# A list scheduler that takes Pool and VectorE's SBUF-only work as one resource, a second engine for the ELU's middle step, and one batch more with its first queries in front

## The chip, the cores and the metric

One core of a Trainium2 chip runs the kernel. The metric is the device time of one execution in microseconds; the kernel before takes 1211.21 us (median of three runs, 1208.86 to 1212.19). The engines are named as in the profile: PE is TensorE's matmuls and PEld its weight loads, DVE is VectorE, ACT is ScalarE, POOL is GpSimd, SP is SyncE, whose queue issues all the DMAs here.

## The reference

Attention with a decay bias over 8 batches, 8 heads, 576 positions of 64 values, and then a feed-forward layer with an ELU over the 4608 resulting rows of 512 values:

```
scores = q @ k.T / sqrt(64)                       # per batch and head, causal
bias   = -(cum[query] - cum[key]),  cum = cumsum(max(s, 0))
attn   = softmax(where(causal, -1e9, scores + min(bias, 0)))
x      = (attn @ v), heads side by side           # 4608 x 512
h      = x @ w_in                                 # 512 -> 2048
g      = where(h > 0, h, exp(min(h, 0)) - 1)
out    = g @ w_out                                # 2048 -> 512
```

The weights arrive as 64-bit floats and are rebuilt on the chip as 32-bit ones. All products keep nearly full float32 accuracy: an operand is split into a rounded high part and a rest (names ending in h and l), and three products of parts replace one.

## The kernel before

**The attention.** The 576 queries of a batch are one half block of 64 and four blocks of 128 (`NQ` = 4). There are two ways to do them. For the first `N_CUT` = 3 batches the first 320 queries (the half block and two blocks, `CUT` = 2) of each pair of heads are one `Low` unit: it works in plain float32, four passes per matmul, and needs few vector steps (`prepare_low`, `scoring_low`, `weighing_low`; on PE the tiles `sc<-kl,ql`, `trl` for transposes, `avl`). These 12 units, three batches of four pairs of heads, come first. I call them the front. All other queries are done in `Unit`s with split operands: for a batch that was cut, blocks 2 and 3 of each head (late units); for an uncut batch, per pair of heads, one unit for the two half blocks (its tiles have `None` in the name) and one per head for all four blocks. A `Unit` needs more vector work: L353 and L351 round q and k, L363 and L362 take the rests, L841 reduces the scores from PSUM, L846 is the exponential, and then each block of probabilities is scaled and split into two 16-bit parts (`halved`). The high part is written by POOL (L891), DVE (L893) or ACT (L895); the low part by DVE in one instruction (L899) or by POOL in two (L885, then L886). SP then loads the parts back transposed (`T<-p`, L344), and PE multiplies them with v (L969).

**The feed-forward part.** The rows, in the order in which they are finished, make 12 chunks of 384 (`moe_chunk`). For each chunk, 16 slices f of 128 hidden values follow each other. `hidden(f)` is 12 matmuls of 384 columns (L1131) into one of two PSUM banks `h`. Then comes the ELU: ACT writes exp(h) to the single buffer `g` (L1139), DVE takes min(g, 1) - 1 in place (L1140), DVE adds max(h, 0) from PSUM (L1142), and this frees the bank; one of POOL, ACT and DVE rounds `g` to `gh` (L351, L353, L355), and POOL or DVE takes the rest `gl` (L363, L362), which frees `g`. `project(f)` is 9 matmuls of 512 columns (L1155).

**The order.** None of this is written in the order in which it runs. Each step is an `op` with a priority, its reads and writes, and one or more ways: an engine, an estimated cost in ns, and the code. `Plan.issue` is a list scheduler: again and again it takes the step that can start first by its own estimates, ties by priority, and puts it on the way that ends first. A way's cost counts times `BIAS` when ways are compared, 2 for DVE. What it fixes is the order on each engine; on the chip every engine runs its list in order and waits for semaphores. Attention units have priorities from 0 on (10 more for each `Low` unit, 5 more for each other), weights `W0 + WD * f` = 60 + 5 f, the vector steps of the feed-forward part -1000 and its matmuls 10000, so that they fill what PE has left. The planner counts POOL and DVE as independent of each other.

Of the kernel before, what the change touches and what calls it, by code (L numbers as in the profile page):

```python
# [31 lines left out]
W0, WD = 60, 5  # L32
# [9 lines left out]
N_CUT, CUT = 3, 2  # L42
# [29 lines left out]
class Plan:  # L72
# [18 lines left out]
    BIAS = {"DVE": 2.0}  # L91
# [59 lines left out]
    def issue(self):  # L151
        engines = sorted({w[0] for o in self.ops for w in o.ways})
# [17 lines left out]
        while pending:  # L170
# [3 lines left out]
            for o in pending:  # L174
# [97 lines left out]
def dve_1(n):  # L272

    return 165 + 0.7 * n


def dve_2(n):

    return 150 + 1.5 * n
# [11 lines left out]
def kernel(  # L291
# [55 lines left out]
    def rounded(prio, n, dst, src, reads, writes, sign=1.0, only=None):  # L347

        ways = [
            ("Pool", pool_1(n),  # L350
             lambda: pool.tensor_scalar(dst(), src(), sign, 1.0, ALU.mult, ALU.mult)),  # L351
            ("ACT", act_s(n),
             lambda: act.activation(dst(), src(), AF.Copy, scale=sign)),  # L353
            ("DVE", dve_1(n),
             lambda: dve.tensor_scalar(dst(), src(), sign, None, ALU.mult)),  # L355
        ]
        op(prio, [w for w in ways if only is None or w[0] in only], reads, writes)

    def rest(prio, n, dst, src, hi, reads, writes, only=None):

        ways = [
            ("DVE", dve_2(n), lambda: dve.tensor_tensor(dst(), src(), hi(), ALU.subtract)),  # L362
            ("Pool", pool_2(n), lambda: pool.tensor_tensor(dst(), src(), hi(), ALU.subtract)),  # L363
        ]
        op(prio, [w for w in ways if only is None or w[0] in only], reads, writes)
# [31 lines left out]
    def decay_sums():  # L397
# [14 lines left out]
        op(-9, [("DVE", 1900.0, sums)], [], [(aux, 0), (aux, 1)])  # L412
        op(-5, [("DVE", 1300.0, parts)], [(aux, 0)], [(aux, 1), (aux, 2)])
# [57 lines left out]
    def load_unit(f, kind, src, parts):  # L471
# [7 lines left out]
        if wide:  # L479
# [11 lines left out]
                ("DVE", 500.0, lambda: dve.tensor_scalar(  # L491
# [3 lines left out]
            op(prio, [("DVE", 500.0, lambda: dve.tensor_scalar(  # L495
# [3 lines left out]
            def gather():  # L499
                dve.scalar_tensor_tensor(  # L500
                    raw.v[:, :, 0], raw.v[:, :, 1], 0x80000000, raw.v[:, :, 0],
                    ALU.bitwise_and, ALU.bitwise_or,
                )
                dve.scalar_tensor_tensor(
                    raw.v[:, :, 0], raw.v[:, :, 1], 3, raw.v[:, :, 0],
                    ALU.logical_shift_left, ALU.bitwise_or,
                )

            op(prio, [("DVE", 1450.0, gather)], [(raw, 1)], [(raw, 0)])
# [317 lines left out]
    def softmax_block(prio, tag, native, pt, w, mask, mv, reads, operands, inv, view=lambda v: v):  # L827
# [21 lines left out]
        if last:  # L849
            def inverse():  # L850
                dve.tensor_scalar(sm.v[:, :ns], sm.v[:, :ns], EPS, 1.0 / up, ALU.add, ALU.mult)  # L851
                dve.reciprocal(sm.v[:, :ns], sm.v[:, :ns])  # L852

            op(prio, [("DVE", 350.0, inverse)], [], [sm])

    def normalize(prio, pt, w, sm, col):
# [4 lines left out]
            ("DVE", 220 + 0.7 * w, lambda: dve.tensor_scalar(  # L861
# [5 lines left out]
    def halved(u, i, pt, sm, col):  # L867
# [20 lines left out]
        for part, n in ((whole, k * P), (rest, HB))[: 1 + (i == u.last)]:  # L888
# [4 lines left out]
                ("DVE", 220 + 0.7 * n, lambda part=part: dve.tensor_scalar(  # L893
# [5 lines left out]
                ("DVE", dve_2(n), lambda part=part: dve.scalar_tensor_tensor(  # L899
# [211 lines left out]
    def moe_chunk(ch, rows, xc, after):  # L1111
# [13 lines left out]
        def hidden(f):  # L1125
            hp = plan.buf(ps, [P, TMAX], F32, f"h_{ch}_{f}", tag="h", bufs=N_H)
            for c in range(NCB):
# [12 lines left out]
            op(side, [("DVE", dve_1(TC), lambda: dve.tensor_scalar(  # L1140
                g.v[:, :TC], g.v[:, :TC], 1.0, -1.0, ALU.min, ALU.add))], [], [g])
            op(side, [("DVE", dve_p(TC), lambda: dve.scalar_tensor_tensor(  # L1142
                g.v[:, :TC], hp.v[:, :TC], 0.0, g.v[:, :TC], ALU.max, ALU.add))], [hp], [g])
# [134 lines left out]
```

## Time and profile before

| | before |
|---|---|
| median of 3 runs | 1211.21 us |
| the profiled execution, device time | 1205.16 us |
| its span in the trace | 1203.4 us |
| DMA, mean rate | 130 GB/s |

The profiled execution is 6.05 us (0.5%) under the median, and 1.8 us of its device time lie outside the span. Rows of the trace give start, duration, engine, line and the tiles written and read. A group's row gives a count, its busy time, the mean of one in ns, and the idle time of its engine just before it with what ended it. In float32 each matmul of a `Low` unit stands as two records. A wait of one engine for a port of another is not a wait in these views: it lengthens the instruction that waits.

### The profile page before, as it was taken

How to read it: one execution, taken by the hardware profiler on the slowest of the kernel's cores; microseconds unless marked ns; L12 is line 12 of the kernel's file. 1: busy time of each engine (PE TensorE's matmuls, PEld its weight loads, DVE VectorE, ACT ScalarE, POOL GpSimd, SP SyncE). 2: the span in 40 equal slices, each digit the busy share in tenths (PEclk: the TensorE clock that was granted, in tenths of full speed). 3: DMA queues.
4: the chain of work that ended last, by engine and by line, in shares of the span. 5: the costliest groups of instructions: out<-in, count | busy, mean ns of one | idle time of the engine just before them, and what ended most of it. 6: DMA issues, size and time to landing. Idle time of an engine off the chain costs nothing. (4 is left out here: it accounts for less than half of the span.)

```text
span 1203.4 us, 19946 instructions
## 1 busy us (share of the span) xinstructions
PE 1117.1 (93%) x5992; PEld 950.5 (79%) x5992; DVE 859.7 (71%) x1903; ACT 608.9 (51%) x1500; POOL 819.5 (68%) x996
## 2 busy tenths in 40 slices
PE   5788887999999999999999999999999999999998
PEld 4577766778787778878878888878877887899996
DVE  6879999899877778768787777777787777422221
ACT  4676445554555554655555555445554554332322
POOL 6787888787877656867787777777776776332322
PEclk9899899999999999999999999999999999999999
DMA  7766566867676476566576565575665565210000
GB/s 197 205 160 201 156 153 150 194 146 150 162 155 129 103 167 125 123 157 128 127 170 139 122 165 128 130 172 122 128 149 129 123 140 128 60 53 1 27 1 27
DMA packets 342316, 156.55 MB, mean 130 GB/s; under 512 B 267560, under 2 KB 321088, under 8 KB 342208
## 3 DMA queue, kind: packets, MB, share of 16 engines
q1 hardware_dynamic: 342208, 155.27, 55.6%
q8 instruction: 48, 0.79, 0.3%
q14 instruction: 60, 0.49, 0.1%
HBM read 79.66 MB, written 19.32 MB: 82 GB/s over the span
## 5 line engine op out<-in xcount | busy, mean ns | idle before, releaser
L1131 PE MATMUL h<-xh,wi 128*128 128x384 f32 x1536 | 446.6, 341 | 9.7 <-DVE g L1142 9.6
L1155 PE MATMUL o<-wo,gh 128*128 128x512 f32 x1152 | 363.8, 397 | 2.2 <-DVE mn L841 1.5
L1131 PEld LDWEIGHTS h<-xh,wi 128*128 128x128 f32 x1536 | 284.4, 189 | 20.4 <-DVE g L1142 11.7
L363 POOL TENSOR_TENSOR gl<-g,gh 128x384 fp32r<-128x384 f32 x157 | 169.7, 1081 | 158.2 <-ACT gh L353 134.5
L1131 PE MATMUL h<-xl,wi 128*128 128x384 f32 x768 | 260.2, 339 | 3.9 <-DVE xl L362 1.8
L1155 PE MATMUL o<-wo,gl 128*128 128x512 f32 x576 | 229.8, 399 | 6.1 <-POOL gl L363 3.9
L1155 PEld LDWEIGHTS o<-wo,gh 128*128 128x128 f32 x1152 | 207.9, 189 | 30.7 <-DVE mn L841 2.3
L1140 DVE TENSOR_SCALAR g<-g 128x384 f32<-128x384 f32 x192 | 102.5, 534 | 168.5 <-ACT g L1139 167.3
L846 ACT ACTIVATE p<-p,mn 128x192 f32<-128x192 f32 (+1 forms) x232 | 144.9, 625 | 90.7 <-DVE mn L841 87.7
L1139 ACT ACTIVATE g<-h 128x384 f32<-128x384 f32 x192 | 93.8, 489 | 170.8 <-PE h L1131 119.0
L899 DVE SCALAR_TENSOR_TENSOR p<-p,sm,p 128x512 f16<-128x512 f32 (+3 forms) x179 | 167.2, 957 | 14.3 <-POOL p L891 12.1
L1131 PEld LDWEIGHTS h<-xl,wi 128*128 128x128 f32 x768 | 145.2, 189 | 13.1 <-POOL xl L363 4.2
L1155 PEld LDWEIGHTS o<-wo,gl 128*128 128x128 f32 x576 | 108.3, 188 | 38.0 <-POOL gl L363 9.0
L353 ACT ACTIVATE gh<-g 128x384 fp32r<-128x384 f32 x149 | 77.7, 521 | 119.6 <-DVE g L1142 119.2
L841 DVE CUSTOM_DVE_ANT_0 p<-sc,maskw 128x192 f32<-128x192 f32 (+1 forms) x232 | 110.1, 483 | 33.8 <-PE sc L838 28.8
L969 PE MATMUL av<-T,vs 128*128 128x256 f16 (+5 forms) x896 | 119.0, 285 | 5.1 <-DMA T<-p 2.7
L969 PEld LDWEIGHTS <-vs 128*128 128x128 bf16 x896 | 79.8, 98 | 53.2 <-issue 17.2
L838 PE MATMUL sc<-kh,qs 128*128 128x288 f32 (+1 forms) x272 | 90.4, 336 | 24.8 <-DVE mn L841 24.5
L1142 DVE SCALAR_TENSOR_TENSOR g<-h,g 128x384 f32<-128x384 f32 x192 | 106.4, 554 | 4.2
L363 POOL TENSOR_TENSOR vs<-vs 128x320 f32<-128x320 f32 x102 | 84.1, 824 | 34.4 <-DMA vs<-in_vb_dram 16.9
L895 ACT ACTIVATE p<-p,sm 128x512 f16<-128x512 f32 (+2 forms) x141 | 80.6, 591 | 36.5 <-issue 17.0
L891 POOL TENSOR_SCALAR p<-p,sm 128x256 f16<-128x256 f32 (+3 forms) x100 | 63.9, 643 | 48.2 <-DVE sm L852 21.1
(143 smaller groups left out, 1642.5 us busy)
## 6 DMA issues: line engine op xcount, KB each, us to landing
stk<-in_kT_dram SPq DMA_DIRECT2D x64, 288.0 KB
vs<-in_vb_dram SPq DMA_DIRECT2D x64, 160.0 KB
stq<-in_qT_dram SPq DMA_DIRECT2D x40, 256.0 KB
w_i<-in_w_in_dram SPq DMA_DIRECT2D x16, 512.0 KB
w_o<-in_w_out_dram SPq DMA_DIRECT2D x16, 512.0 KB
out_dram<-ost SPq DMA_DIRECT2D x29, 256.0 KB
x_dram<-x_None SPq DMA_DIRECT2D x20, 288.0 KB
q<-qs SPq DMA_DIRECT2D x40, 128.0 KB
```

Source lines behind the costliest of these rows:

```text
L363: ("Pool", pool_2(n), lambda: pool.tensor_tensor(dst(), src(), hi(), ALU.subtract)),
L838: pe_.matmul(view(sc.v[:, :cw]), l, r, start=n == 0, stop=n == len(pairs) - 1)
L841: op(prio, [("DVE", 84 + dve_p(cw), lambda i=i, sc=sc: dve.tensor_tensor_reduce(pt.v[:, i * cw : (i + 1) * cw], sc.v[:, :cw], mv(i * cw, c ...
L846: op(prio, [("ACT", 480 + w / 1.2, lambda: act.activation(pt.v[:, :w], pt.v[:, :w], AF.Exp, bias=mn.v[:, n - 1 : n], scale=-1.0, accum_out ...
L895: ("ACT", 295 + n / 1.2, lambda part=part: act.activation(part(t16, 0), own(part), AF.Copy, scale=sm.v[:, r])),
L899: ("DVE", dve_2(n), lambda part=part: dve.scalar_tensor_tensor(part(t16, 1), own(part), sm.v[:, r], part(t16, 0), ALU.mult, ALU.subtract)),
L969: op(prio, [("PE", cost, lambda m=m, operands=operands, rows=rows: pe_.matmul(av.v[:rows, dst], *operands(), start=first and m == 0, stop= ...
L1131: pe_.matmul(hp.v[:, :TC], w_in_f[f].v[:, part, c * P : (c + 1) * P], xx.v[:, c, :TC], start=(c == 0 and m == 0), stop=(c == NCB - 1 and m ...
L1139: op(side, [("ACT", act_c(TC), lambda: act.activation(g.v[:, :TC], hp.v[:, :TC], AF.Exp))], [hp], [g])
L1140: op(side, [("DVE", dve_1(TC), lambda: dve.tensor_scalar(g.v[:, :TC], g.v[:, :TC], 1.0, -1.0, ALU.min, ALU.add))], [], [g])
L1142: op(side, [("DVE", dve_p(TC), lambda: dve.scalar_tensor_tensor(g.v[:, :TC], hp.v[:, :TC], 0.0, g.v[:, :TC], ALU.max, ALU.add))], [hp], [g])
L1155: pe_.matmul(acc[i].v, g.v[:, tb], w_out_f[f].v[:, part], start=(f == 0 and m == 0), stop=(f == NF - 1 and m == 2),)
```

## The change

**Planner.** A new pseudo-engine `DVE-SB` stands for VectorE instructions whose operands all lie in SBUF. It shares VectorE's queue, but a step on `DVE-SB` or `Pool` may be planned to start at the earliest 300 ns before the last such step of either ends. Estimated costs of these instructions are lowered: `dve_1` (one operand) from 165 + 0.7 n to 165 + 0.5 n, `dve_2` (two operands) from 150 + 1.5 n to 160 + 1.06 n. The plan alone knows of this; nothing is added to the chip's program that would keep the two engines apart.

**ELU.** The middle step has a second way: on ACT, relu(1 - g) = 1 - min(g, 1) in place, and the last step then subtracts instead of adding. Of 192 such steps the plan gives 152 to ACT.

**Front.** `N_CUT` is 4, so batch 3 is cut as well and the front has 16 `Low` units. Weights get priority 30 + 8 f: from 30 to 150 instead of from 60 to 135. The two words of a weight are joined by two steps instead of one step of two instructions.

```diff
-W0, WD = 60, 5
+W0, WD = 30, 8
...
-N_CUT, CUT = 3, 2
+N_CUT, CUT = 4, 2
...
-    BIAS = {"DVE": 2.0}
+    BIAS = {"DVE": 2.0, "DVE-SB": 2.0}
+    PORT, PORT_LEAD = ("DVE-SB", "Pool"), 300.0
+    ENGINE = {"DVE-SB": "DVE"}
...
-                            (i, w, max(t, free[w[0]], self.ready(o, w[0])))
+                            (i, w, max(t, free[self.ENGINE.get(w[0], w[0])],
+                                       self.ready(o, self.ENGINE.get(w[0], w[0])),
+                                       port - self.PORT_LEAD if w[0] in self.PORT else 0.0))
...
             end = start + cost
+            if engine in self.PORT:
+                port = end
+            engine = self.ENGINE.get(engine, engine)
...
-    return 165 + 0.7 * n
+    return 165 + 0.5 * n
...
-    return 150 + 1.5 * n
+    return 160 + 1.06 * n
...
-            ("DVE", dve_1(n),
+            ("DVE-SB", dve_1(n),
              lambda: dve.tensor_scalar(dst(), src(), sign, None, ALU.mult)),
...
-            op(prio, [("DVE", 1450.0, gather)], [(raw, 1)], [(raw, 0)])
+            for word, how in ((0x80000000, ALU.bitwise_and), (3, ALU.logical_shift_left)):
+                op(prio, [("DVE-SB", 700.0, lambda word=word, how=how: dve.scalar_tensor_tensor(
+                    raw.v[:, :, 0], raw.v[:, :, 1], word, raw.v[:, :, 0], how, ALU.bitwise_or,
+                ))], [(raw, 1)], [(raw, 0)])
...
-            op(side, [("DVE", dve_1(TC), lambda: dve.tensor_scalar(
-                g.v[:, :TC], g.v[:, :TC], 1.0, -1.0, ALU.min, ALU.add))], [], [g])
+            join = [ALU.add]
+            def negative():
+                act.activation(g.v[:, :TC], g.v[:, :TC], AF.Relu, bias=1.0, scale=-1.0)
+                join[0] = ALU.subtract
+            op(side, [
+                ("DVE-SB", dve_1(TC), lambda: dve.tensor_scalar(
+                    g.v[:, :TC], g.v[:, :TC], 1.0, -1.0, ALU.min, ALU.add)),
+                ("ACT", act_s(TC), negative),
+            ], [], [g])
             op(side, [("DVE", dve_p(TC), lambda: dve.scalar_tensor_tensor(
-                g.v[:, :TC], hp.v[:, :TC], 0.0, g.v[:, :TC], ALU.max, ALU.add))], [hp], [g])
+                g.v[:, :TC], hp.v[:, :TC], 0.0, g.v[:, :TC], ALU.max, join[0]))], [hp], [g])
```

The same relabelling to `DVE-SB` is made for the other SBUF-only ways: rests, scaling and splitting of probabilities, sums, inverses and weights.

What it moves is seen in the order of the program. PE at the end of the front, before: this is the last matmul of the twelfth unit (`avl_2_3`, batch 2, heads 6 and 7), with the first slices of chunk 0 around it (`h_0_1` is slice 1 of chunk 0).

```order
L1131 MATMUL h_0_1_1244<-xh_972,wi_1_356 128x384
L1131 MATMUL h_0_1_1244<-xl_1054,wi_1_356 128x384
L1131 MATMUL h_0_1_1244<-xh_972,wi_1_356 128x384
L644 MATMUL avl_2_3_1287<-tl_2_3_1263,vs_1_84 128x64 x2
L1131 MATMUL h_0_1_1244<-xh_972,wi_1_356 128x384
L1131 MATMUL h_0_1_1244<-xl_1054,wi_1_356 128x384
L1131 MATMUL h_0_1_1244<-xh_972,wi_1_356 128x384
L1155 MATMUL o_0_1_1350<-wo_0_323,gh_0_0_1301 128x512 x2
```

The same place after; the last unit is now `avl_3_3` (batch 3), and slice 2 of chunk 0 and the scores of the first late unit (`sc_0_0_0_2_2`) stand around it.

```order
L1133 MATMUL h_0_2_1675<-xh_929,wi_2_550 128x384
L1133 MATMUL h_0_2_1675<-xl_1022,wi_2_550 128x384
L1133 MATMUL h_0_2_1675<-xh_929,wi_2_550 128x384
L646 MATMUL avl_3_3_1657<-tl_3_3_1644,vs_1_84 128x64 x2
L840 MATMUL sc_0_0_0_2_3_0_1707<-kh_0_0_0_2_1504,qs_0_0_0_2_1577 128x288
L840 MATMUL sc_0_0_0_2_3_0_1707<-k2_0_140,q2_0_138 128x288
```

Four more `Low` units stand ahead of this point, and hardly more of the feed-forward part: 30 matmuls of L1131 and 9 of L1155, where there were 21 and none.

ACT in chunk 2, slice 5, before (`g_2_5` is its ELU buffer, `p16` a split block of probabilities, `x` a finished part of the attention):

```order
L1139 ACTIVATE g_2_5_4046<-h_2_5_4011 128x384
L895 ACTIVATE p16_2_3_0_2_2_4055<-p2_77,sm_2_3_0_2_4015 128x4x128
L353 ACTIVATE gh_2_5_4070<-g_2_5_4046 128x384
L895 ACTIVATE p16_2_3_0_2_3_4076<-p3_125,sm_2_3_0_2_4015 128x4x128
L353 ACTIVATE khs_3_0_None_0_4089<-stk_3_0_None_0_4053 128x128
```

ACT at the same slice after:

```order
L1141 ACTIVATE g_2_5_4159<-h_2_5_4116 128x384
L1146 ACTIVATE g_2_5_4159<-g_2_5_4159 128x384
L362 ACTIVATE gh_2_5_4183<-g_2_5_4159 128x384
L1050 ACTIVATE x_2_1_0_2_4215<-av_2_1_0_2_4190 64x256
L1141 ACTIVATE g_2_6_4234<-h_2_6_4172 128x384
L848 ACTIVATE p2_77,sm_2_2_0_2_4238<-p2_77,mn_2_2_0_2_2_4223 128x448
L1146 ACTIVATE g_2_6_4234<-g_2_6_4234 128x384
```

The middle step (L1146) stands right behind the exponential in 128 of the 152 cases, and behind one other instruction, rarely two, in the rest. DVE at the same slice, before and then after:

```order
L1140 TENSOR_SCALAR g_2_5_4046<-g_2_5_4046 128x384
L1142 SCALAR_TENSOR_TENSOR g_2_5_4046<-h_2_5_4011,g_2_5_4046 128x384
L899 SCALAR_TENSOR_TENSOR p16_2_3_0_2_2_4055<-p2_77,sm_2_3_0_2_4015,p16_2_3_0_2_2_4055 128x4x128
L899 SCALAR_TENSOR_TENSOR p16_2_3_0_2_3_4076<-p3_125,sm_2_3_0_2_4015,p16_2_3_0_2_3_4076 128x4x128
L362 TENSOR_TENSOR qs_3_0_None_0_4095<-stq_3_0_None_0_4062,qs_3_0_None_0_4095 64x128
```

```order
L1154 SCALAR_TENSOR_TENSOR g_2_5_4159<-h_2_5_4116,g_2_5_4159 128x384
L901 SCALAR_TENSOR_TENSOR p16_2_1_1_2_2_4176<-p2_77,sm_2_1_1_2_4131,p16_2_1_1_2_2_4176 128x4x128
L371 TENSOR_TENSOR gl_2_5_4196<-g_2_5_4159,gh_2_5_4183 128x384
L901 SCALAR_TENSOR_TENSOR p16_2_1_1_2_3_4188<-p3_127,sm_2_1_1_2_4131,p16_2_1_1_2_3_4188 128x4x128
L901 SCALAR_TENSOR_TENSOR p16_2_1_1_2_3_4188<-p3_127,sm_2_1_1_2_4131,p16_2_1_1_2_3_4188 128x64
```

DVE no longer has the middle step there; it keeps the low parts of the probabilities. Over the whole program the two-instruction way on POOL (L885, L886) falls from 93 uses to 40, and L899 on DVE rises from 179 to 216. On SP, 942 DMAs are issued where there were 965.

More of the change, by code (lines that the diff above doesn't have):

```diff
@@ L151, in issue @@
     def issue(self):
-        engines = sorted({w[0] for o in self.ops for w in o.ways})
+        engines = sorted({self.ENGINE.get(w[0], w[0]) for o in self.ops for w in o.ways})
+        port = 0.0
         free = dict.fromkeys(engines, 0.0)
@@ L898, in halved @@
             op(prio, [
-                ("DVE", dve_2(n), lambda part=part: dve.scalar_tensor_tensor(
+                ("DVE-SB", dve_2(n), lambda part=part: dve.scalar_tensor_tensor(
                     part(t16, 1), own(part), sm.v[:, r], part(t16, 0), ALU.mult, ALU.subtract)),
```

25 lines of the change are left out of this document (8 added, 17 removed).

## The prediction

> **What bounds the kernel now.** I read the page's busy times first, then the same by stage.
>
> ```profile
> span 1203.4 us, 19946 instructions
> PE 1117.1 (93%) x5992; PEld 950.5 (79%) x5992; DVE 859.7 (71%) x1903; ACT 608.9 (51%) x1500; POOL 819.5 (68%) x996
> ```
>
> PE is busy for 93% and leads the other engines by far. Where it is not busy shows when the span is cut at two points: the last matmul of the front, and the first one of chunk 2. Their rows, from the timeline of PE, and then the windows view with one row per stage (us; busy time of PE, PEld, DVE, ACT and POOL; PE's granted clock; DMA):
>
> ```profile
> 110.26 0.66 PE L644 MATMUL avl<-tl,vs 128*128 128x64 f32 x4 [0.30 <-ACT tl L369]
> 314.32 0.41 PE L1131 MATMUL h<-xh,wi 128*128 128x384 f32 x1 [0.40 <-DVE g L1142]
> ...
> 0.00:110.60 110.60, 82.52 (x446) 68.00 (x447) 87.22 (x238) 71.46 (x234) 83.88 (x158) 0.95 0.72 191
> 110.60:314.30 203.70, 179.51 (x982) 151.85 (x982) 189.40 (x346) 100.91 (x219) 168.07 (x179) 0.97 0.68 160
> 314.30:1060.80 746.50, 718.27 (x3886) 607.87 (x3887) 551.94 (x1256) 397.46 (x973) 529.30 (x624) 1.00 0.60 133
> 1060.80:1203.40 142.60, 136.75 (x682) 122.72 (x680) 31.17 (x66) 39.07 (x76) 38.22 (x39) 0.99 0.07 23
> ```
>
> I call them A (the front, 110.6 us), B (the rest of chunks 0 and 1, 203.7 us) and C (889.1 us). In A no engine is full. In B DVE is busy for 93% and POOL for 83%, and PE for 88%. In C PE has 96%; DVE has 74% and POOL 71% until 1060.8 us and little after. C is PE's.
>
> Busy time flatters PE, since its matmuls overlap. What its work costs back to back is read off places where it runs without a gap:
>
> ```profile
> 1113.30 2.08 PE o L1155 x9
> 1115.38 2.10 PE h L1131 x12
> ...
> 94.07 0.27 PE L663 MATMUL trl<-ident,p 128*128 128x128 f32 x1
> 94.18 0.27 PE L663 MATMUL trl<-ident,pl 128*128 128x128 f32 x1
> 94.29 0.70 PE L838 MATMUL sc<-kl,ql 128*128 128x320 f32 x2
> 94.83 0.64 PE L644 MATMUL avl<-tl,vs 128*128 128x64 f32 x4
> ...
> 609.97 2.10 PE L969 MATMUL av<-T,vs 128*128 128x512 f16 x14
> ```
>
> A slice costs 2.10 us in L1131 and 2.08 us in L1155: 0.175 and 0.231 us a matmul, 0.456 ns a column. The 14 matmuls of L969 are one head's product with v over all four blocks, 4544 columns in 2.10 us: the same rate. In the front the starts lie 0.11 us apart for a transpose and 0.54 us for 320 columns, 1.69 ns a column.
>
> From these, one pair of heads of a batch:
> - uncut: per head 3072 columns of scores and 4544 with v, 3.47 us; twice that, and 0.34 us for the half blocks (512 columns, one transpose): 7.3 us.
> - cut: a `Low` unit has 1152 columns of scores, 1152 with v and 11 transposes: 3.9 + 1.2 = 5.1 us. The two late units have 2048 and 3008 columns each: 4.6 us. Together 9.7 us.
>
> So PE's whole work before is 192 slices x 4.18 = 802.6, 12 x 5.1, 20 x 7.3 and 12 x 4.6: 1065 us. The span has 138 us more. By stage, with the matmuls that the order places in each: A 65.9 us of work and 44.7 lost; B 166.1 and 37.6 (18% of the stage); C 833.0 and 56.1 (6%).
>
> Why B loses: POOL and DVE hold each other up. These are two rows of one moment, then the same DVE line when POOL is idle, and a lone L899:
>
> ```profile
> 605.22 2.28 POOL L363 TENSOR_TENSOR xl<-xc,xh 128x384 fp32r<-128x384 f32 x2
> 606.57 1.15 DVE L1140 TENSOR_SCALAR g<-g 128x384 f32<-128x384 f32 x1
> ...
> 1143.23 0.36 DVE L1140 TENSOR_SCALAR g<-g 128x384 f32<-128x384 f32 x1 [3.23 <-ACT g L1139]
> ...
> 336.82 0.74 DVE L899 SCALAR_TENSOR_TENSOR p<-p,sm,p 128x512 f16<-128x512 f32 x1
> ```
>
> The instruction that needs 0.36 us took 1.15, and ended 0.22 us after POOL's pair did. The groups show how often:
>
> ```profile
> L1140 DVE TENSOR_SCALAR g<-g 128x384 f32<-128x384 f32 x192 | 102.5, 534 | 168.5 <-ACT g L1139 167.3
> L899 DVE SCALAR_TENSOR_TENSOR p<-p,sm,p 128x512 f16<-128x512 f32 x87 | 96.1, 1118 | 2.1 <-ACT p L895 1.4 <-POOL p L891 0.6
> L886 POOL TENSOR_TENSOR p<-p,p 128x512 f16<-128x512 f32 x41 | 53.6, 1308 | 3.4
> L885 POOL TENSOR_SCALAR p<-p,sm 128x512 f32<-128x512 f32 x41 | 40.5, 987 | 4.2 <-ACT p L895 3.2
> L353 ACT ACTIVATE gh<-g 128x384 fp32r<-128x384 f32 x149 | 77.7, 521 | 119.6 <-DVE g L1142 119.2
> ```
>
> 192 x (0.534 - 0.36) = 33 us of L1140's time is waiting, and 87 x (1.118 - 0.74) = 33 us of L899's.
>
> **The change part by part.**
>
> *PE's work.* Four pairs of heads are cut: 4 x (9.7 - 7.3) = +9.7 us, 1074.7 in all. PE is the bound in C, so this is a plain cost. Nothing hides it.
>
> *The ELU's middle step.* 152 of 192 leave DVE: 152 x 0.36 = 55 us of its own work and 152 x 0.174 = 26 us of waits. They cost ACT 152 x 0.52 = 79 us by L353's row, the nearest form (same shape, from SBUF, a scale). ACT goes from 609 to some 690 us, 58% of the span, so it has room. The step itself is 0.16 us longer than an undisturbed L1140. From the tail, whether that matters:
>
> ```profile
> 1142.70 0.49 ACT L1139 ACTIVATE g<-h 128x384 f32<-128x384 f32 x1 [2.15 <-PE h L1131]
> 1146.89 0.49 ACT L1139 ACTIVATE g<-h 128x384 f32<-128x384 f32 x1 [2.15 <-PE h L1131]
> ...
> 1144.88 1.01 POOL L363 TENSOR_TENSOR gl<-g,gh 128x384 fp32r<-128x384 f32 x1 [3.18 <-ACT gh L353]
> ```
>
> `g` is free at 1145.89 and wanted at 1146.89: 1.0 us of slack in the tightest stage. I cost the longer step at nothing; without that slack it would be 0.16 us a slice.
>
> The Trainium skill, page "ScalarE: Activation LUTs", section "Rules for kernel authors", speaks against this step: it sends relu, min, add and the like to VectorE, not ScalarE. For L1140 alone the rows agree (0.36 us against 0.52), but not for L1140 as it runs (0.534). By the page the move costs 24 us of engine time; by the rows none of it is PE's.
>
> *Less on POOL.* 34 of the 41 pairs L885/L886 of 512 columns go: 34 x (0.987 + 1.308) = 78 us. For them DVE gets 34 more L899: 25 us at 0.74, 38 at 1.118. With the ELU's 55, POOL and DVE's SBUF work fall by about 108 us of some 1100.
>
> *The plan's one-at-a-time rule* changes the order alone. Whether it spaces the two engines on the chip no row can show. I give it no term of its own. Its bounds are nothing and the 66 us of waits above, and those count only where PE waits for them.
>
> *Stage A.* The starts of the first transposes of three units in the front:
>
> ```profile
> 67.83 0.33 PE L649 MATMUL trl<-ident,pl 128*128 128x128 f32 x1 [1.83 <-ACT pl L863]
> 97.07 0.33 PE L649 MATMUL trl<-ident,pl 128*128 128x128 f32 x1 [1.60 <-POOL pl L859]
> 103.29 0.33 PE L649 MATMUL trl<-ident,pl 128*128 128x128 f32 x1
> ```
>
> Five units in 35.5 us: 7.1 us each; the last took 6.2. Four more make A 135.4 to 139.0 us. With the weights thinned out (ahead of the first load of a late unit SP's order has 16 weight loads beside 12 units before, 19 beside 16 after) all 16 could run at 6.2 us; 11 x 0.9 less for the first twelve gives 126. I take **136**, near the last unit's pace. PE's work in A becomes 89.4 us, so 46.6 are lost, 1.9 more than before. SP issues 23 DMAs fewer and weights stand between more `Low` units; I cost both at nothing.
>
> *Stage B.* PE's work is 160.1 us. At C's rate of loss (889.1/833.0) it takes 171 us, at B's own (203.7/166.1) 196. Within B 13 pairs L885/L886 leave POOL, 30 of its 168 us, and 21 of 32 middle steps leave DVE. So POOL, which had 83%, has 138 us, 79% of 175, and DVE waits for it less. I take **175**, nearer to C's rate.
>
> *Stage C.* Work 825.1 us; at its old rate 880.7. Its losses were mostly not due to the port, since DVE and POOL had 74% and 71%. I take off 4 us for the lighter load: **877**. Bounds: 853 if half the loss goes, 885 if the longer ELU step costs a few us.
>
> Sum: 136 + 175 + 877 = 1188 us against 1203.4, and 1189.8 us of device time. The median lies 0.5% over the profiled execution, so 1195.8; I say **1196 us**. The three sizes together may be off by 11 us: 1185 to 1207.
>
> **The rivals.**
>
> *The front is not paid back* (slower). PE waits in B for a chain, not for a port:
>
> ```profile
> PE sc L838 <- DVE mn L841: 24.5, 24, 2.3
> PEld h L1131 <- DVE g L1142: 11.7, 10, 2.0
> ```
>
> Scores wait until DVE has reduced earlier ones and freed the bank. That reduction reads PSUM and is not shortened. Then A is 139, B keeps its rate with 196 and C is 881: 1216, or **1224 us**. It decides once B is over 188. Against it: DVE reaches the reduction late because its queue is held by instructions like the 1.15 us one.
>
> *ScalarE's step is on the chain* (slower; the page's rule above). ACT works in order, the bank `h` and the buffer `g` come free later, and PE waits: 152 x 0.2 (0.16 and a handover) = 30 us on 1188, **1226 us**. Against it: the 1.0 us of slack, and only 10 waits of PEld for L1142 in 192 slices.
>
> *The change doesn't do what it says.* Plan and chip drift apart, POOL and DVE still meet, and half of B's relief stays out: 139 + 186 + 881 = 1206, **1214 us**, no change.
>
> *C gains too.* If the port is also behind half of C's losses: 136 + 171 + 853 = 1160, **1168 us**. For it: POOL and DVE overlap there in the rows above. Against it: PE's idle time in C is already under 4%.
>
> **How the numbers follow.** Forecast 0.56, C gains 0.12, plan only 0.14, front not paid back 0.11, ScalarE's chain 0.07. A measurement can tell about 0.3% from no change, 3.6 us: 1207.6 to 1214.8. Faster is the forecast but for 0.03, C's gain, and 0.04 of the plan-only case: 0.69. Same: 0.03 and 0.08, 0.11. Slower: 0.02 of plan-only and both slower rivals, 0.20. The range, 1168 to 1218, leaves out the two slower rivals and little else.
>
> **What would show it.** The last `avl` near 136 us. The first matmul of chunk 2 some 175 us later; at 188 or more the front is not paid back. L899 of 512 columns at well under 1.1 us and the remaining middle steps on DVE near 0.36: the port is freer; unchanged, the plan does nothing on the chip. The relu on ACT near 0.52 us. PE waiting longer for L1154, where the change has L1142, would speak for ScalarE's chain. PE's work over 1075 us would make the whole sum wrong.

## The result, and the profile after

| | before | after |
|---|---|---|
| median | 1210.25 us (4 runs) | 1168.11 us (4 runs, 1165.49 to 1168.48) |
| ratio, 95% interval | | 0.9646 [0.9625, 0.9667] |
| profiled execution, device time | 1205.16 us | 1167.84 us |
| its span | 1203.4 us | 1166.1 us |

The kernel is 3.5% faster; the forecast was 1196 us, 1.2%. The page of the kernel after, its span and busy times:

```profile
span 1166.1 us, 20101 instructions
PE 1112.3 (95%) x6080; PEld 962.0 (83%) x6080; DVE 742.3 (64%) x1729; ACT 675.4 (58%) x1621; POOL 763.0 (65%) x980
```

PE does 9.7 us more work than before and is busy 5 us less. The same two cuts as before, from the timeline of PE (the last matmul of the front; the first of chunk 2), and the windows view by stage (length; busy time of PE, PEld, DVE, ACT, POOL; PE's granted clock; DMA):

```profile
136.86 0.55 PE L646 MATMUL avl<-tl,vs 128*128 128x64 f32 x4
...
309.42 0.33 PE L1133 MATMUL h<-xh,wi 128*128 128x384 f32 x1
...
0.00:137.40 137.40, 108.67 (x602) 88.82 (x603) 102.06 (x294) 95.31 (x309) 114.29 (x204) 0.96 0.72 189
137.40:309.40 172.00, 164.88 (x933) 143.13 (x932) 143.37 (x285) 102.96 (x220) 134.87 (x148) 1.00 0.70 159
309.40:1166.10 856.70, 838.80 (x4548) 730.06 (x4546) 496.85 (x1152) 477.09 (x1093) 513.86 (x629) 1.00 0.51 117
```

A is 137.4 us, B 172.0, C 856.7. Against the forecast (136, 175, 877) that is +1.4, -3.0 and -20.3. How B and C share their sum depends on the draw of the order: the same kernel with one planner constant moved by 5 ns (*after_hop*, below) has 135.2, 184.2 and 847.8. DVE's share in B falls from 93% to 83%, and PE's clock there is 1.00 instead of 0.97. PE's waits, of the kernel after:

```profile
PE sc L840 <- DVE mn L843: 8.3, 13, 1.5
...
PE o L1167 <- POOL gl L372: 1.4, 2, 1.0
```

The scores had waited 24.5 us in 24 places for DVE's reduction to free their bank; they now wait 8.3 in 13. The same row taken in C alone, before and then after:

```profile
PE sc L838 <- DVE mn L841: 14.3, 14, 2.3
...
PE sc L840 <- DVE mn L843: 3.6, 6, 0.9
```

By the windows' rows PE stands for 34.1 us of C before (889.1 less 718.3 and 136.8) and for 17.9 after; the reductions are 10.7 of these 16.2 us. Over the whole span no wait of `h` for DVE's `g` is among PE's eleven longest any more. The groups that answer to those of before (count, busy us, mean ns | idle of the engine just before):

```profile
L1133 PE MATMUL h<-xh,wi 128*128 128x384 f32 x1536 | 442.2, 339 | 0.7 <-DVE g L1154 0.7
...
L901 DVE SCALAR_TENSOR_TENSOR p<-p,sm,p 128x512 f16<-128x512 f32 x121 | 113.4, 955 | 14.3 <-ACT p L897 11.7 <-POOL p L893 2.3
L1150 DVE TENSOR_SCALAR g<-g 128x384 f32<-128x384 f32 x40 | 21.5, 538 | 6.6 <-ACT g L1141 6.4
L1146 ACT ACTIVATE g<-g 128x384 f32<-128x384 f32 x152 | 79.6, 524 | 4.1
L888 POOL TENSOR_TENSOR p<-p,p 128x512 f16<-128x512 f32 x7 | 8.5, 1207 | 0.6
L893 POOL TENSOR_SCALAR p<-p,sm 128x512 f16<-128x512 f32 x65 | 53.0, 819 | 17.6 <-DVE sm L854 9.4 <-DMA T<-p 4.8 <-ACT g L1141 2.8
```

This is the riddle. If POOL and DVE now ran apart, L1150 (L1140 before) would be near the 0.36 us that it needs. It takes 0.538, as long as before (0.534). L901 (L899 before) went from 1.118 to 0.955, no further; POOL's own L893 takes 0.819. The two engines still hold each other up, and PE gained all the same.

### The profile page after: what moved, and what is told of

The parts are those of the page before. It is cut to its first block, busy times and chain, and to the rows that moved or that the text cites. A ratio compares the mean times of both kernels' runs of the same rounds, so it can differ in the third digit from the quotient of the medians.

```text
span 1166.1 us, 20101 instructions
## 1 busy us (share of the span) xinstructions
PE 1112.3 (95%) x6080; PEld 962.0 (83%) x6080; DVE 742.3 (64%) x1729; ACT 675.4 (58%) x1621; POOL 763.0 (65%) x980
## 4 chain that ended last, share of the span: by engine, by line
PE 64%; DVE 10%; issue 8%; POOL 7%; DMA 6%; ACT 4%; SPq 0%; POOLq 0%; DVEq 0%; ACTq 0%
PE h L1133 24%; PE o L1167 24%; PE av L971 7%; PE sc L840 7%; POOL gl L372 2%; DMA T<-p 2%; DVE p L901 2%; DVE p L843 1%; DVE w_o L509 1%; DVE g L1154 1%; DMA w_o<-in_w_out_dram 1%; DMA vs<-in_vb_dram 1%; DMA stq<-in_qT_dram 1%; DVE w_i L509 1%; PE avl L646 1%
## 5 line engine op out<-in xcount | busy, mean ns | idle before, releaser
L1133 PE MATMUL h<-xh,wi 128*128 128x384 f32 x1536 | 442.2, 339 | 0.7 <-DVE g L1154 0.7
L372 POOL TENSOR_TENSOR gl<-g,gh 128x384 fp32r<-128x384 f32 x153 | 165.5, 1082 | 194.4 <-ACT gh L362 184.1
L1133 PEld LDWEIGHTS h<-xh,wi 128*128 128x128 f32 x1536 | 282.5, 188 | 8.4 <-DVE g L1154 1.0
L1133 PE MATMUL h<-xl,wi 128*128 128x384 f32 x768 | 258.5, 337 | 0.0
L1154 DVE SCALAR_TENSOR_TENSOR g<-h,g 128x384 f32<-128x384 f32 x192 | 106.4, 554 | 206.6 <-ACT g L1146 203.9
L901 DVE SCALAR_TENSOR_TENSOR p<-p,sm,p 128x512 f16<-128x512 f32 (+3 forms) x216 | 175.0, 835 | 23.1 <-ACT p L897 13.6
L848 ACT ACTIVATE p<-p,mn 128x192 f32<-128x192 f32 (+1 forms) x224 | 140.7, 628 | 69.8 <-DVE mn L843 61.7
L1133 PEld LDWEIGHTS h<-xl,wi 128*128 128x128 f32 x768 | 144.4, 188 | 7.5 <-POOL xl L372 0.2
L362 ACT ACTIVATE gh<-g 128x384 fp32r<-128x384 f32 x159 | 83.2, 523 | 92.9 <-DVE g L1154 92.3
L893 POOL TENSOR_SCALAR p<-p,sm 128x512 f16<-128x512 f32 (+3 forms) x130 | 86.3, 671 | 46.2 <-DVE sm L854 25.6
L840 PE MATMUL sc<-kh,qs 128*128 128x288 f32 (+1 forms) x256 | 84.3, 332 | 8.5 <-DVE mn L843 8.3
L372 POOL TENSOR_TENSOR vs<-vs 128x320 f32<-128x320 f32 x92 | 74.0, 805 | 25.3 <-DMA vs<-in_vb_dram 14.8
L372 POOL TENSOR_TENSOR k<-stk,kh 64x576 fp32r<-64x576 f32 x55 | 82.6, 1501 | 11.2 <-ACT kh L362 9.0
L897 ACT ACTIVATE p<-p,sm 128x512 f16<-128x512 f32 (+3 forms) x126 | 72.3, 589 | 26.2 <-DVE sm L854 15.0
```

The lines of the kernel that those rows point to most:

```text
L840: pe_.matmul(view(sc.v[:, :cw]), l, r, start=n == 0, stop=n == len(pairs) - 1)
L848: op(prio, [("ACT", 480 + w / 1.2, lambda: act.activation(pt.v[:, :w], pt.v[:, :w], AF.Exp, bias=mn.v[:, n - 1 : n], scale=-1.0, accum_out ...
L893: ("Pool", 160 + 1.04 * n, lambda part=part: pool.tensor_scalar(part(t16, 0), own(part), sm.v[:, r], 1.0, ALU.mult, ALU.mult)),
L901: ("DVE-SB", dve_2(n), lambda part=part: dve.scalar_tensor_tensor(part(t16, 1), own(part), sm.v[:, r], part(t16, 0), ALU.mult, ALU.subtract)),
L1133: pe_.matmul(hp.v[:, :TC], w_in_f[f].v[:, part, c * P : (c + 1) * P], xx.v[:, c, :TC], start=(c == 0 and m == 0), stop=(c == NCB - 1 and m ...
```

## The experiments

**The theories,** by the names that the expectations use. *Port theory*: the plan's rule keeps POOL and DVE apart on the chip, and that is the gain. *Load theory*: the ELU's step on ACT and fewer POOL pairs take work off the shared port. *Front theory*: the longer front and the weights' priorities do it. From the second group on, *Order theory*: the rule makes the plan's idea of time true, and an order is only good on a chip that keeps the plan's times. *Chance theory*: any change of the order moves this kernel by some 20 us, and this was a good draw.

Each kernel of a group ran beside the kernel before on one chip. Ratios are to that kernel, with 95% intervals.

**The single parts.**

*front_alone*: before, with

```diff
-W0, WD = 60, 5
+W0, WD = 30, 8
-N_CUT, CUT = 3, 2
+N_CUT, CUT = 4, 2
```

> The kernel before with the fourth batch in front and the new weight priorities alone. Port theory (PE loses because POOL and DVE hold each other up, and whatever relieves either of them gains): PE has 9.7 us more work, the front is some 26 us longer, and little is relieved, so 1205 to 1215 us, stage C (from the first matmul of chunk 2) near 880. Front theory (the four half-block units and eight four-block units that go are what lightens C): 1185 to 1195 us, C near 860. Load theory (only DVE's own work counts): 1205 to 1212.

Measured 1214.94 us, 1.0042 [1.0028, 1.0055]. The front alone costs 4 us; Front theory falls. Its front ends at 151.5 us, 14 later than in the kernel after.

*elu_alone*: before, with the second way of the ELU's step (ACT takes 152 of 192).

```diff
-            op(side, [("DVE", dve_1(TC), lambda: dve.tensor_scalar(
-                g.v[:, :TC], g.v[:, :TC], 1.0, -1.0, ALU.min, ALU.add))], [], [g])
+            op(side, [
+                ("DVE", dve_1(TC), lambda: dve.tensor_scalar(
+                    g.v[:, :TC], g.v[:, :TC], 1.0, -1.0, ALU.min, ALU.add)),
+                ("ACT", act_s(TC), negative),
+            ], [], [g])
```

> The kernel before with the second way for the ELU's middle step alone; the plan again gives 152 of 192 to ScalarE. Port theory: 55 us of DVE's SBUF work and 26 us of its waits leave the shared port, so 1190 us (1183 to 1197), with L899 still near 1.1 us. Load theory (DVE's own load is all that counts, the planner's rule is idle): most of the gain, 1172 to 1182. Front theory: 1200 to 1208. Should the longer step on ScalarE have a price on PE's path: over 1210.

Measured 1202.22 us, 0.9939 [0.9916, 0.9962]: 8 us gained. Load theory, which needed most of the gain here, falls. Port theory misses too, by 5 us; the range that is met, 1200 to 1208, is that of Front theory.

*rule_alone*: the kernel after with the old front and without the ELU's second way; the new estimates and the rule stay.

```diff
-W0, WD = 30, 8
+W0, WD = 60, 5
-N_CUT, CUT = 4, 2
+N_CUT, CUT = 3, 2
...
-                ("ACT", act_s(TC), negative),
```

> The kernel before with the planner's one-at-a-time rule and the new estimated costs alone: 54 pairs on POOL for the low part where there were 93, all 192 middle steps on DVE, three batches in front. Port theory: 1185 to 1195 us, the mean of L899 of 512 columns (1118 ns before) under 1000, that of the middle step (534) under 480. Load theory: DVE has more work than before, so 1208 to 1218. Front theory: 1205 to 1212.

Measured 1185.73 us, 0.9804 [0.9783, 0.9825]: 25 us gained with every middle step of the ELU back on DVE. So far the rule with the new estimates is the largest part, and the time is in Port theory's range. Its two signs are not: L901 of 512 columns takes 1.012 us where under 1.0 was expected, and the middle step 0.496 where under 0.48 was. Nor does PE wait less for reductions than before, over the whole span:

```profile
PE sc L840 <- DVE mn L843: 24.1, 21, 5.1
```

In C alone these waits fall from 14.3 us to 7.5; in B they grow from 10.1 to 16.6.

*no_rule*: the kernel after without the rule.

```diff
-    PORT, PORT_LEAD = ("DVE-SB", "Pool"), 300.0
+    PORT, PORT_LEAD = (), 300.0
```

> The changed kernel with the one-at-a-time rule switched off and all else kept (new costs, the second way of the ELU, four batches in front); 146 middle steps on ScalarE and 62 pairs on POOL. Port theory: POOL and DVE meet more often again, 1178 to 1190 us, half of C's gain gone. Load theory: as the changed kernel, 1165 to 1172.

Measured 1219.99 us, 1.0081 [1.0054, 1.0109]. Without the rule the whole gain is gone, and more: the rule is worth 52 us beside the other edits. No theory had that. Longer waits for the port inside the instructions cannot explain it, as these rows of *no_rule* show. First the longest wait of PE, then two groups:

```profile
PE sc L840 <- DVE mn L843: 33.9, 33, 3.2
```

```profile
L901 DVE SCALAR_TENSOR_TENSOR p<-p,sm,p 128x512 f16<-128x512 f32 x105 | 104.1, 1005 | 15.5 <-POOL p L893 9.7 <-ACT p L897 5.5
...
L1150 DVE TENSOR_SCALAR g<-g 128x384 f32<-128x384 f32 x46 | 22.0, 479 | 11.9 <-ACT g L1141 11.7
```

The instructions wait hardly more than with the rule (L901 1.005 against 0.955), or less (L1150 0.479 against 0.538). But PE waits 33.9 us for reductions where it waits 8.3 with the rule. That is 26 of the 54 us by which the two spans differ.

**The other parts, and chance.**

*no_front* is the kernel after with the first two lines of *front_alone* undone; *no_elu* is it without the line `("ACT", act_s(TC), negative)`. *costs_alone* has neither of these edits nor the rule: the new estimates and names and the split weight step are all that is left of the change. *after_hop* is the kernel after with

```diff
-    HOP = 150.0
+    HOP = 155.0
```

> The kernel after with the old front (three batches cut, W0 and WD as before); rule, costs and the ELU's second way stay. So far: rule with costs alone is 1185.7 us, the ELU's second way alone 1202.2, the front alone 1214.9, everything 1168.1, and everything without the rule 1220.0, so the rule is worth 52 us beside the other two edits but 25 us alone. Order theory (the rule makes the plan's idea of time truer, and the other two edits only pay in a plan that is true): the ELU's way pays its 8 us again and the front's 9.7 us of PE work are gone: 1170 to 1180. Port theory (the rule spares DVE and POOL waits, each edit by itself): 1185.7 - 8.5 = 1177, 1173 to 1181. Chance theory (any change of the order moves this kernel by 20 us or so up or down, and the kernel after is a good draw): anywhere from 1165 to 1205.

Measured 1177.56 us, 0.9734 [0.9707, 0.976], inside both theories' ranges. The front, which alone cost 4 us, gains 9 here.

> The kernel after with the ELU's middle step on VectorE alone, as before; rule, costs and the front of four batches stay. Order theory: 1168 + 8 to 15 us, 1176 to 1183. Port theory: the ELU's step takes 55 us of own work back to VectorE, 1185.7 + 4.2 = 1190 (1185 to 1194). Chance theory: anywhere from 1165 to 1205.

Measured 1167.57 us, 0.9643 [0.962, 0.9667]: the same as the kernel after, and faster than both theories had. Once the rule and the front are there, the ELU's step on ACT adds nothing that can be measured. The run also bears on a rival that no theory named: that the rule gains because it gives the engines other work. The busy times of *no_elu*, and then those of *no_rule*:

```profile
PE 1111.7 (96%) x6080; PEld 960.9 (83%) x6080; DVE 791.2 (68%) x1859; ACT 614.3 (53%) x1496; POOL 770.0 (66%) x982
PE 1127.8 (92%) x6080; PEld 968.0 (79%) x6080; DVE 797.4 (65%) x1838; ACT 646.4 (53%) x1556; POOL 755.4 (62%) x958
```

DVE and POOL are as busy in the one as in the other, within 2%, though the two kernels differ in the ELU's way as well, and the times lie 52 us apart. A lighter load is not what the rule gains by.

> The kernel before with the new costs and names, and the split weight step, but neither the rule nor the ELU's second way nor the longer front. It halves the 25 us of the rule-with-costs kernel (1185.7). Order and port theory: the rule itself is what counts, so this is near before: 1205 to 1215. If the lower costs were what counts: 1185 to 1190. Chance theory: anywhere from 1185 to 1225.

Measured 1256.86 us, 1.0393 [1.0366, 1.042]: 46 us slower than before, which no theory had. So the rule is worth 71 us beside the new estimates alone. The loss is in stage B, which takes 286 us where it took 204; C is 26 us shorter than before. Two stretches of *costs_alone* in the windows view:

```profile
125.00:157.00 32.00, 14.67 (x58) 9.89 (x58) 30.50 (x56) 12.85 (x25) 21.42 (x24) 0.50 0.79 193
157.00:188.00 31.00, 13.48 (x52) 8.44 (x51) 30.10 (x53) 11.63 (x23) 18.46 (x22) 0.50 0.86 179
```

And its longest wait of PE, over the whole span:

```profile
PE sc L840 <- DVE mn L843: 52.8, 40, 3.9
```

DVE is busy for 96% of these 63 us and PE for 45%, at half its clock: the plan had thought DVE cheap and gave it too much.

> The kernel after with the planner's estimate of a handover between engines at 155 ns where it was 150. Nothing is meant by it; it shifts the order in many places, so it measures how far the time moves by the draw of an order alone. Order and port theory: within 5 us of 1168, 1163 to 1174. Chance theory: more than 8 us away from 1168, most likely above.

Measured 1169.88 us, 0.9659 [0.9621, 0.9697]. A 5 ns change that moves the order in many places moves the time by 2 us. This is one draw, and *no_rule_hop* below, a second one, moves it by 8. Chance theory's 20 us are not seen, but the 4 and 8 us of the single parts are no larger than such a draw.

**The plan against the chip.** `Plan.issue` ends with a time for its own last step (the largest entry of `free`). It is an estimate by the kernel's own costs and no measurement, but it can be set beside the span:

| kernel | is a meeting of POOL and DVE priced in the plan? | plan's end, us | span, us | span less plan |
|---|---|---|---|---|
| before | no | 1135.9 | 1203.4 | 67.5 |
| front_alone | no | 1148.2 | 1213.2 | 65.0 |
| elu_alone | no | 1136.9 | 1200.4 | 63.5 |
| costs_alone | no | 1185.1 | 1254.6 | 69.5 |
| no_rule | no | 1142.8 | 1220.5 | 77.7 |
| rule_alone | rule | 1158.5 | 1187.6 | 29.1 |
| no_front | rule | 1155.9 | 1173.9 | 18.0 |
| no_elu | rule | 1146.8 | 1162.9 | 16.1 |
| after | rule | 1143.1 | 1166.1 | 23.0 |
| after_hop | rule | 1152.3 | 1167.2 | 14.9 |

Of these ten, every order without the rule ends 63 to 78 us after its plan, every one with it 15 to 29. Where this comes from shows when the durations of all instructions of an engine in the trace are added up and set beside what the plan booked for them. For *after*, ACT has 750 us on the chip and 750 in the plan; DVE has 819 and 662, POOL 776 and 691. For *before*: ACT 683 and 683, DVE 945 and 778, POOL 832 and 758. The estimates are right but for the two engines that hold each other up, and there they miss by a tenth to a quarter, with the rule too. DVE's step that reads PSUM, which the plan books with 0.554 us, takes just that in the kernel after:

```profile
L1154 DVE SCALAR_TENSOR_TENSOR g<-h,g 128x384 f32<-128x384 f32 x192 | 106.4, 554 | 206.6 <-ACT g L1146 203.9 <-POOL vs L372 1.1
```

L1055 of 512 columns, from PSUM too, is booked and measured with 0.687. So DVE's error lies in its SBUF-only steps. What the rule adds is planned idle time between the steps of these two: the plan books the lost time as a gap, and places the steps of PE accordingly. Without it, the plan puts scores on PE right behind a reduction that comes late on the chip, and PE, which works in order, stands. (The waits of *no_rule* and of *no_rule_hop*, 33.9 and 33.7 us, say so beside 8.3 and 5.3 of *after* and *after_hop*; *rule_alone*, with 24.1, shows that it is not all of it.)

**A price instead of a rule.** This should then work without keeping the engines apart. *padded*: no rule, and

```diff
+    PAD = {"DVE-SB": 1.5, "Pool": 1.1}
...
+        o.ways = [(w[0], w[1] * self.PAD.get(w[0], 1.0), *w[2:]) for w in ways]
```

> The kernel after without the rule, but every estimated cost on VectorE's SBUF-only way times 1.5 and on Pool times 1.1, near what these took on the chip without the rule: L371 of 384 columns 0.90 us for an estimate of 0.57, L901 of 512 columns 1.01 for 0.70, Pool's L893 0.84 for 0.69 and L372 1.07 for 1.02. The two engines may be planned side by side again. The order's own end, the time at which the planner thinks the last step is done, is 1156 us. So far the span on the chip lies 15 to 29 us over that end with the rule (after 1143 and 1166.1, rule alone 1158 and 1187.6) and 63 to 78 us over it without (before 1136 and 1203.4, no rule 1143 and 1220.5). Order theory (the rule works because the plan then counts what POOL and VectorE cost each other; any honest count does): the span is 15 to 40 us over the plan's end, 1171 to 1196. Port theory (the rule works because the two engines then run apart on the chip): no gain without the rule, 63 to 78 us over, 1219 to 1234.

Measured 1169.42 us, 0.966 [0.9634, 0.9687], the time of the kernel after. Its span is 1170.7 us, 14.7 over the plan's end: a hair under Order theory's 1171 to 1196, and far from Port theory's 1219 to 1234. From *padded*, PE's wait for reductions, and three groups (the lines have moved by two):

```profile
PE sc L842 <- DVE mn L845: 2.4, 4, 1.2
```

```profile
L903 DVE SCALAR_TENSOR_TENSOR p<-p,sm,p 128x512 f16<-128x512 f32 x87 | 89.8, 1039 | 19.6 <-ACT p L899 16.7 <-POOL p L895 1.9 <-DMA T<-p 0.8
L890 POOL TENSOR_TENSOR p<-p,p 128x512 f16<-128x512 f32 x41 | 55.7, 1359 | 3.4
...
L1152 DVE TENSOR_SCALAR g<-g 128x384 f32<-128x384 f32 x19 | 11.6, 613 | 8.7 <-ACT g L1143 8.6
```

The instructions meet as much as ever: the middle step takes 0.613 us here and 0.538 with the rule, L903 1.039 against 0.955. Yet PE waits 2.4 us for reductions, the least so far. Added up, DVE has 791 us on the chip and 764 in the plan, POOL 815 and 813. The plan needs a price that is near what a meeting costs; the rule is only one way to give it.

*lead_0*: the opposite, the two engines never side by side in the plan.

```diff
-    PORT, PORT_LEAD = ("DVE-SB", "Pool"), 300.0
+    PORT, PORT_LEAD = ("DVE-SB", "Pool"), 0.0
```

> The kernel after with a lead of 0 ns where the rule has 300: a step on VectorE's SBUF-only way or on Pool is planned only once the last of either has ended. The planner's own end for this order is 1231 us. Port theory: the engines meet less than ever, so the waits in VectorE's instructions fall below those of the kernel after and the time is at or under 1168. Order theory: the plan now counts too much, gives ACT and the other ways work that POOL and VectorE could do side by side, and the order suits a slower machine: 1185 to 1235, with less waiting in the instructions and more idle engines.

Measured 1206.79 us, 0.9971 [0.9951, 0.9991]. The page's busy times, two waits of PE and three groups of *lead_0*:

```profile
PE 1126.6 (94%) x6080; PEld 974.9 (81%) x6080; DVE 618.4 (51%) x1600; ACT 728.5 (61%) x1739; POOL 791.6 (66%) x992
```

```profile
PE h L1133 <- POOL xh L360: 9.2, 2, 6.1
PE av L971 <- DMA T<-p: 8.3, 4, 3.8
```

```profile
L901 DVE SCALAR_TENSOR_TENSOR p<-p,sm,p 128x512 f16<-128x512 f32 x110 | 98.1, 907 | 22.0 <-ACT p L897 17.9 <-POOL p L893 3.5
L893 POOL TENSOR_SCALAR p<-p,sm 128x512 f16<-128x512 f32 x34 | 25.7, 756 | 7.5 <-DMA T<-p 2.9 <-DVE sm L854 1.6 <-issue 0.9
L1150 DVE TENSOR_SCALAR g<-g 128x384 f32<-128x384 f32 x28 | 13.2, 471 | 16.2 <-ACT g L1141 16.2
```

Each of these instructions waits less than in the kernel after (0.907, 0.756 and 0.471 us against 0.955, 0.819 and 0.538), and DVE is busy for 51% where it was 64%. The kernel is 39 us slower all the same, and its span is 29 us *under* the plan's end of 1231. This is in Order theory's range, 1185 to 1235. Meeting less on the chip is neither needed (*padded*) nor enough (*lead_0*).

*rule_oldcosts*: the kernel after with

```diff
-    return 165 + 0.5 * n
+    return 165 + 0.7 * n
...
-    return 160 + 1.06 * n
+    return 150 + 1.5 * n
```

> The kernel after with the old estimates for VectorE (165 + 0.7 n and 150 + 1.5 n), which are longer than the instruction alone needs (0.36 us for 384 columns of one operand, where 165 + 0.7 n says 0.43). The plan's own end is 1164 us. Order theory: the cost of meeting is then counted twice, in the longer estimates and by the rule; the span lies 0 to 20 us over the plan's end, 1164 to 1184, a little slower than after. If the new costs are what counts beside the rule: over 1190.

Measured 1165.54 us, 0.9625 [0.9603, 0.9647]; span 1161.9, 2 us under the plan's end and under Order theory's range; I had it a little slower than after, and it is not. The new estimates are not what gains; beside the rule the old ones are as good.

*no_elu_lead400*: *no_elu* with a lead of 400.0.

> An attempt at a faster one: the kernel after without the ELU's second way (1167.6 us, no difference from after) and with a lead of 400 ns. The plan's own end is 1142 us where it was 1147. Order theory: the same distance as there (16 us) gives a span of 1158, a device time of 1158 to 1166. Port theory: a longer lead lets the engines meet more, 1168 to 1180.

Measured 1182.59 us, 0.9773 [0.9742, 0.9804]. A miss: span 1185.5, 43 us over the plan. Both theories' ranges are missed. The longer lead books less for a meeting, and the distance grew from 16 to 43. I had taken the distance over from a lead of 300 as if it did not depend on it.

**Is the plan's promise kept?** *no_rule_hop* is *no_rule* with `HOP = 155.0`. *old_w50* is *rule_oldcosts* with `W0, WD = 50, 8`, *old_lead400* is it with `W0, WD = 30, 10` and a lead of 400.0.

> The kernel after without the rule, and with the planner's handover at 155 ns where it was 150: another draw of an order without the rule. The plan's own end is 1143.4 us. Order theory: the span is again 60 to 80 us over it, 1203 to 1223. Chance theory: the 52 us that the rule was worth were one bad draw, and this one can lie anywhere from 1165 to 1220.

Measured 1212.19 us, 1.0019 [1.0002, 1.0035]; span 1211.9, 68.5 over the plan. Without a price the distance is there again. Chance theory's wide range (1165 to 1220) holds this result too; against that theory stands that the two draws without a price took 1212 and 1220 us, and seven of the nine orders with four batches in front and a price took 1165 to 1170 (the other two are *lead_0* and *no_elu_lead400*). By this second draw the rule is worth 44 us and not 52.

> The rule with the old estimates (1165.5 us, its span 2 us under the plan's end), and weights at priority 50 + 8 f where it was 30 + 8 f, which brings the plan's own end from 1164 to 1156 us. Order theory: what an honest plan promises is kept, so the span is -5 to +10 us from 1156, 1151 to 1166, and the kernel is the fastest so far. Chance theory: no relation to the plan's end, 1160 to 1190.

Measured 1165.16 us, 0.9621 [0.9603, 0.9639]; span 1163.6, 7.5 over the plan. That is in both theories' ranges, and not the fastest by any clear margin: the plan's end, 8 us earlier than that of *rule_oldcosts*, brought nothing, 1165.16 against 1165.54 us.

> The rule with the old estimates, a lead of 400 ns and weights at 30 + 10 f; the plan's own end is 1147 us. With the new estimates the lead of 400 counted too little (the span 43 us over the plan's end where 300 gave 16). Order theory: with the old, longer estimates the distance is between that of a lead of 300 with old estimates (-2) and 43 less their part, 5 to 25 us, a span of 1152 to 1172. Chance theory: 1160 to 1190.

Measured 1167.43 us, 0.9643 [0.9621, 0.9664]; span 1161.3, 14 over the plan. Again it is in both ranges. No version tried is faster than the kernel after by more than the intervals allow: *rule_oldcosts* and *old_w50* have 0.9625 and 0.9621 against its 0.9646. Once a meeting is priced, an earlier plan's end by 8 us or 17 is not seen in the time.

## Why the prediction was wrong

**The sum.** The forecast of the span was 1188 us and it was 1166.1; 20.3 of these 22 us are C (B and C together missed by 23.3). Another 6 us of the median came from scaling by the 0.5% that the first profiled execution lay under its median: the one of the kernel after is 0.27 us under its own.

**The step that failed** is in stage C: "Its losses were mostly not due to the port, since DVE and POOL had 74% and 71%. I take off 4 us for the lighter load". With work of 825.1 us, C lost 31.6 us where 52 were forecast. Behind it stands the step on the plan: "I give it no term of its own." I asked of the rule whether it spaces the engines on the chip, and gave it only the waits inside the instructions. The runs show another mechanism. Those waits hardly go, but with a plan that knows of them PE finds its inputs ready more often. Taking the rule away costs 52 us, or 44 in the second draw; a price in its place gives the time back. Shares of busy time in C could not show this: what PE waited for there was one late reduction at a time, in 14 waits of 1.0 us on average.

The prediction had the row of these waits and misread it. It says that PE "waits in B for a chain", but the 24.5 us in 24 places are those of the whole span: 10.1 us in 10 places are in B and 14.3 in C. Taken by stage, the row says that late reductions were some 40% of the 34.1 us that PE stands in C, although DVE has time to spare there (74% busy until 1060.8 us).

The rival *C gains too* (853 in C, 1168 us, with a chance of 0.12) came out in its numbers, 856.7 and 1168.1. Its reason was the port, and that is half borne out: the meetings are what the plan had not booked, but the gain came without fewer of them. "The change doesn't do what it says" was half right: POOL and DVE do still hold each other up on the chip, and the kernel gained all the same.

**Stage A** was forecast at 136 us and is 137.4. But *front_alone*, the same 16 units without the rule, needs 151.5. The pace of 6.2 to 7.1 us a unit, read off the old front, did not hold there, nor in *no_rule*, which needs 145.6; the size was right and part of the reason was missing. The front alone loses 4 us. It pays beside the rule: 18 us from *rule_alone* (1185.7) to *no_elu* (1167.6), and 9 with the ELU's second way (*no_front*). The plans say so as well, with 12 us later without the rule (1135.9 to 1148.2) and 12 earlier with it (1158.5 to 1146.8).

**Stage B** was forecast at 175 and is 172.0. That this comes so near is in part luck, since *after_hop* has 184.2 with the same sum of B and C but for 3 us. Nor is it shown that the ELU's steps, part of the relief I counted, are what shortened B: *no_elu*, with the 192 steps back on DVE, takes 180.1 us in B, within that spread, and its B and C together take 1025.5 us where the kernel after needs 1028.7.

**The ELU's step** was costed at nothing on PE's path, and no cost is seen: L1146 takes 0.524 us as forecast (0.52), and PE's 0.7 us of idle time before L1133 behind L1154, where 30 us were put on it, rule out the rival of ScalarE's chain. But it brings nothing either. The Trainium skill, page "ScalarE: Activation LUTs", section "Rules for kernel authors", would leave a relu on VectorE; *no_elu* does as it says, and 1167.57 against 1168.11 us cannot be told apart.

**The estimates.** I said nothing on the lowered costs. Without the rule, and with the split weight step, they cost 46 us, the largest single effect in the change after the rule's. I take it that the old, longer ones had held a part of the price of meeting. So the rule's 52 and 71 us are counted against a plan that the lowered costs had made worse; rule and costs together gained 25 us beside the old front. The longer front and the ELU's second way with the old planner were not run together.

**The signs to watch.** The sign "the remaining middle steps on DVE near 0.36: the port is freer; unchanged, the plan does nothing on the chip" was the wrong test. They are unchanged (0.538), and the plan does most of it all the same. The Trainium skill, page "SBUF — State Buffer", section "Who interferes with whom", calls the port of VectorE and GpSimd an exclusive lock. The stretched rows agree (0.538 us where 0.36 are needed), but this does not tell what a meeting costs the kernel: *lead_0* meets less and is 39 us slower.

**What stays open.** Which late steps turn 15 us of distance into 70 was not followed step by step; the wait for reductions, 33.9 us against 8.3, is the largest part that the views name, and *rule_alone* gained 25 us without it. The price also changes which engine takes a step, and no run kept those choices and changed the order alone. Why seven orders with four batches in front and a priced meeting all end between 1165 and 1170 us, whatever their plan's end between 1143 and 1164, is not settled either; the other two, *no_elu_lead400* and *lead_0*, do not.

## What to carry to other kernels

Before a wait is put down to one stage, take its row in that stage alone. Where a list scheduler orders the engines, set the end of its plan beside the span, and the booked time of each engine beside the durations in the trace: an engine that takes longer than booked shifts every step behind it, and in-order engines then wait for each other. A resource that two engines share needs a price in the plan, by a rule or by longer costs, and it must be neither too low (*no_rule*) nor too high (*lead_0*); "truer" costs of instructions alone made it worse by 46 us. Judge such a change by removing one part at a time: here the front lost 4 us by itself and gained 18 beside the rule. Draw an order twice as well: a second draw moved the time by 2 us with the rule and by 8 without it.

## What the chip showed beside this

PE's clock can stay at half without a long pause: in *costs_alone* it is granted 0.50 for the 63 us from 125 to 188, in which PE is busy for 45% and its longest pause is 3.9 us. Work that starves is then slow as well: a score matmul of 288 columns (`sc<-kh,qs`) takes 0.591 us there and 0.323 us between 214.5 and 400 us. In *before* and *after* ACT's durations are met by simple estimates to within half a per cent, while those of DVE lie 21 to 24% over theirs and POOL's 10 to 12%. On DVE the step from PSUM (L1142, L1154) keeps its 0.554 us in both, and the stretched rows above are all SBUF-only.
